# Splitting a 3136-point transform as 49 by 64 instead of 56 by 56 in a spectral layer with a gated feed-forward network

## The chip, the cores and the metric

The kernel runs on one core of a Trainium2 chip. The metric is the device time of one execution in microseconds (us), as the median over several runs. Engines: TensorE (PE; its weight loads are PEld), VectorE (DVE), ScalarE (ACT), GpSimd (POOL), and SyncE (SP), which issues the DMAs.

## The reference

The input x is 8 batches x 3136 positions x 256 channels, in float32. The output has the same shape.

```python
X = np.fft.rfft(x, axis=1)                  # along the 3136 positions
Yr = Xr @ w_r - Xi @ w_i + b_r              # complex 256 x 256 mix of the channels
Yi = Xr @ w_i + Xi @ w_r + b_i
Y = sign(Y) * max(abs(Y) - 0.01, 0)         # soft threshold, real and imaginary part apart
y = np.fft.irfft(Y, n=3136, axis=1)
h = max(y @ w_in, 0)                        # 256 -> 1024
c = depthwise 3-tap convolution of h along the positions (conv_w)
out = (h * sigmoid(c)) @ w_out              # 1024 -> 256
```

The feed-forward weights come as 64-bit floats. The kernel reads them as pairs of 32-bit words and makes two float32 parts of each.

## The kernel before

The transform over 3136 positions is done as two shorter ones, R = 56 rows by 56 columns. Row n, column j is position 56 n + j. *Stage 1* transforms over the rows, *stage 2* over the columns, *mix* multiplies the channels by the complex matrix, *shrink* is the soft threshold, *stage 3* goes back over the columns and *stage 4* over the rows. All of them are matmuls on TensorE except shrink.

**The two units of work.** A *piece* is the work of stage 1 (or of stage 4) on four columns of the first half with their four partners of the second half (`JC = 4`), so 56/8 = 7 pieces a batch and 56 in all. A *unit* is four of a batch's indices u (`UG = 4`); the real input leaves U = 28 indices, so 7 units a batch and 56 in all. Index 0 is special, since it is its own mirror image: in the kernel before it is packed with the other self-mirrored frequency as a unit member with 57 rows instead of 56.

**The way of the data.** A piece of x is loaded by two DMAs of 56 rows x 1024 floats (`load_x`, tile `xr`), goes through `quads` (four matmuls, each on one quadrant of the array: 64 rows by 64 columns), is copied to `a1` by ACT and DVE, and is stored to a scratch in DRAM, `sc1`. A unit is loaded from there (`load_a2`, tile `a2`, 112 rows), goes through `stage2` (8 matmuls), which writes a high part `fh` and a low part `fl`; `third` makes the third column of both (ACT and POOL). `mix` has 36 matmuls over three combinations. `shrink` takes two ACT instructions and one on POOL. `stage3_pe` has 8 matmuls on quadrants; `stage3_out` copies the result to `z1` (ACT) and stores it to a second scratch, `sc2`. Stage 4 loads from it a piece of 8 columns (`load_z2`), runs 8 matmuls and copies a high and a low part to `yh` and `yl`, which the feed-forward stage reads. The profile often shows two records for one such matmul (16 for the 8 of stage 2).

**The order.** Up to the feed-forward stage the order of every engine is that of the code: one loop, `for it in range(n_it + LAG)`, in which iteration `it` does stage 3 of unit it - 4, a piece of stage 1 of a later batch, stage 2 of unit `it`, shrink of unit it - 2, `third` of unit `it`, and mix of unit it - 1. Ahead of the loop stands the *head*, which does the pieces of batch 0. The last iterations, from `n_it` on, are the *drain*: no new units come. In five iterations near the end and in two of the drain a stage 4 of batch 0 is done (`Y0`, `Y1`), so that the feed-forward stage can start. All DMAs are issued by SP, in the order of the code; a DMA that has to wait holds up those behind it. The generator `later()` (`background`) loads and splits the weights of the feed-forward stage during the loop, a few instructions each iteration. It also loads the table of stage 4 (`i2`, from `in_inv`) and the three convolution taps (`cw`, by `load_bits`, L244 before). `load_inv1` loads the tables of stage 3, `load_t2` those of stage 2, `load_mix` the mixing weights `wm_raw`.

At a *batch boundary* the first unit of a batch needs the last piece of that batch: its store to `sc1`, then the load of `a2`.

The feed-forward stage goes over all positions in pieces of 448 columns: `up` (L542), relu (L544), taps (L547 to L551), sigmoid (L552), gate (L553 to L557), `down` (L570), and the store. The stage-4 pieces of batches 1 to 7 run between its matmuls. There a scheduler sets the order.

Of the kernel before, what the change touches and what calls it, by code (L numbers as in the profile page):

```python
# [18 lines left out]
R = 56  # L19
U = 28  # L20
SL = 57
SP = 64
H = 28
LAM = 0.01
UG = 4
NG = U // UG
JC = 4
P = 128
# [6 lines left out]
def _tables():  # L35
    n = np.arange(R)
    u = np.arange(U)

    f = np.zeros((R, 2, U))
    ang = 2 * np.pi * ((n[:, None] * u[None, :]) % R) / R  # L40
    f[:, 0, :] = np.cos(ang)
    f[:, 1, :] = -np.sin(ang)
    f[:, 1, 0] = np.where(n % 2 == 0, 1.0, -1.0)
    fwd1 = np.zeros((2, SP, SP))
    fwd1[:, :R, :R] = f.transpose(0, 2, 1).reshape(R, R)

    fwd2 = np.zeros((2, R, U, 2, SP))
    inv1 = np.zeros((U, 2, SP, SP))
    jj = np.arange(1, H)
    for uu in range(U):  # L50
        for s in range(SL):
            if uu == 0:
                c = 0 if s < 29 else 1
                k = R * s if s < 29 else 28 + R * (s - 29)
                th = 2 * np.pi * ((k * n) % S) / S
                sn, cs = np.sin(th), np.cos(th)
                edge = k in (0, S // 2)
                if edge:
                    sn = np.zeros(R)
                    cs = np.round(cs)  # L60
                w = 1.0 if edge else 2.0
                fwd2[c, :, 0, 0, s] = cs
                fwd2[c, :, 0, 1, s] = -sn
                inv1[0, 0, s, c:R:2] = w * cs[:H]
                inv1[0, 1, s, 2 + c:R:2] = w * sn[jj]
                if c == 0:
                    inv1[0, 0, s, R] = w * cs[H]
                else:
                    inv1[0, 1, s, 1] = w * sn[H]
            elif s < R:  # L70
                k = uu + R * s
                th = 2 * np.pi * ((k * n) % S) / S
                sn, cs = np.sin(th), np.cos(th)
                sg = 1.0 if k <= S // 2 else -1.0
                fwd2[0, :, uu, 0, s] = cs
                fwd2[1, :, uu, 0, s] = sn
                fwd2[0, :, uu, 1, s] = -sn * sg
                fwd2[1, :, uu, 1, s] = cs * sg
                for c, q in ((0, 1.0), (1, sg)):
                    inv1[uu, c, s, 0] = q  # L80
                    inv1[uu, c, s, 1] = q * (1.0 if s % 2 == 0 else -1.0)
                    inv1[uu, c, s, 2:R:2] = q * cs[jj]
                    inv1[uu, c, s, 3:R:2] = q * sn[jj]

    inv2 = np.zeros((2, 2, 2, U, 2, R))
    for h in range(2):
        for uu in range(U):
            for first in range(2):
                o = inv2[first, :, :, uu, h]
                m = n + (h if not first else 0)  # L90
                if uu == 0:
                    alt = np.where(m % 2 == 0, 1.0, -1.0)
                    if first:
                        o[0, h], o[1, h] = ((1.0, alt), (1.0, -alt))[h]
                        if h:
                            o[0, 0], o[1, 0] = 0.0, 0.0
                            o[0, 1], o[1, 1] = 1.0, -alt
                        else:
                            o[0, 0], o[1, 0] = 1.0, alt
                            o[0, 1], o[1, 1] = 0.0, 0.0  # L100
                    else:
                        sgn = (-1.0, 1.0)[h]
                        o[0, 0], o[1, 0] = 1.0, alt
                        o[0, 1], o[1, 1] = sgn, sgn * alt
                else:
                    th = 2 * np.pi * ((uu * m) % R) / R
                    if first:
                        th = th + h * 2 * np.pi * uu / (2 * R)
                        o[h, 0], o[h, 1] = 2 * np.cos(th), -2 * np.sin(th)
                    else:  # L110
                        sgn = (-1.0, 1.0)[h]
                        o[0, 0], o[1, 0] = 2 * np.cos(th), sgn * 2 * np.sin(th)
                        o[0, 1], o[1, 1] = -2 * np.sin(th), sgn * 2 * np.cos(th)
    order = [g * UG + 2 * k + kk for g in range(NG) for kk in range(2) for k in range(UG // 2)]
    inv2 = inv2[:, :, :, order] / S

    return {
        "fwd1": fwd1.reshape(2 * SP, SP).astype(np.float32),
        "fwd2": fwd2.reshape(2, 2, H, U * 2 * SP).transpose(0, 2, 1, 3).reshape(2 * R, U * 2 * SP).astype(np.float32),
        "inv1": inv1.reshape(U // 2, 2, 2, SP, SP).transpose(1, 3, 0, 2, 4).reshape(2 * SP, U * SP).astype(np.float32),  # L120
        "inv2": inv2.transpose(1, 2, 3, 0, 4, 5).reshape(2 * R, 2 * 2 * R).astype(np.float32),
    }
# [3 lines left out]
def spectral_ffn_kernel(ctx: ExitStack, tc: tile.TileContext, x, w_r, w_i, b_r, b_i,  # L126
                        w_in, conv_w, w_out, fwd1, fwd2, inv1, inv2, out):
    nc = tc.nc
    K1, K2 = 2 * R, 2 * SP

    dram = ctx.enter_context(tc.tile_pool(name="dram", bufs=1, space=DRAM))
    sc1 = [dram.tile([R, 2 * H, D], F32, name=f"sc1_{b}") for b in range(B)]
    sc2 = [dram.tile([H, 4, U, D], F32, name=f"sc2_{b}") for b in range(B)]
# [52 lines left out]
    with ExitStack() as ab:  # L186
# [13 lines left out]
        t2 = c1.tile([K1, U, K2], F32, name="t2")  # L200
# [4 lines left out]
        inv1v = inv1.rearrange("p (u c m) -> p u c m", u=U // 2, c=2)  # L205
        fwd2v = fwd2.rearrange("p (u m) -> p u m", u=U)
# [8 lines left out]
        def load_t2(g):  # L215
            nc.sync.dma_start(t2[:, g * UG:(g + 1) * UG, :], fwd2v[:, g * UG:(g + 1) * UG, :])
# [62 lines left out]
        def later():  # L279
# [12 lines left out]
            bits = [load_bits(conv_w[k].rearrange("(f p) w -> p f w", p=P), NF, "cw", bufs=1, tag=f"cw{k}") for k in range(3)]  # L292
            ask(0)
            yield None
            for n in range(len(pieces)):
                if n + 1 < len(pieces):
                    ask(n + 1)
                yield from split_weight(*asked.pop(0))
# [4 lines left out]
        def load_x(pool, b, jc, **kw):  # L303

            xr = pool.tile([P, JC, D], F32, name="xr", **kw)
            xv = x[b].rearrange("(n h j) d -> h n j d", h=2, j=H)
            for h in range(2):
                nc.sync.dma_start(xr[SP * h:SP * h + R], xv[h, :, jc * JC:(jc + 1) * JC, :])  # L308
# [9 lines left out]
        def store_a1(b, jc, a1):  # L318
            dst = sc1[b].rearrange("m (c r j) d -> r c m (j d)", r=2, j=4)
            for r in range(2):  # L320
                nc.sync.dma_start(dst[r, jc], a1[SP * r:SP * r + R].rearrange("p j h d -> p (j h d)"))
# [15 lines left out]
        def load_a2(b, g):  # L337
            a2 = a2p.tile([K1, UG, D], F32, name="a2")
            ld = nc.sync.dma_start(a2, sc1[b].rearrange("(u c) j d -> (c j) u d", c=2)[:, g * UG:(g + 1) * UG, :])
            return a2  # L340

        def stage2(g, a2):
# [3 lines left out]
            for t in range(NT):  # L346
                ps = psx.tile([P, UG, 2, SP], F32, name="ps_s2", tag="bank")
                for k in range(UG):
                    nc.tensor.matmul(ps[:, k], a2[:, k, t * P:(t + 1) * P], t2[:, g * UG + k, :],  # L349
# [34 lines left out]

        def shrink(v):
# [6 lines left out]
        def stage3_pe(g, r):  # L392
            ps = psa.tile([P, 2, UG // 2, D], F32, name="ps_s3")
            for k in range(UG // 2):
                for h in range(2):
                    for c in range(2):
                        rows = slice(SP * h, SP * (h + 1))
                        nc.tensor.matmul(ps[SP * c:SP * (c + 1), h, k, :], i1[rows, g * UG // 2 + k, c, :], r[rows, c, k, :],  # L398
                                         start=(k == 0), stop=(k == UG // 2 - 1), skip_group_check=True)
            return ps  # L400

        def stage3_out(b, g, ps):
            z1 = io.tile([P, 2, UG // 2, D], F32, name="z1", bufs=2)
            nc.scalar.copy(z1, ps)
            z1 = z1.rearrange("p h k e -> p (h k) e")
            dst = sc2[b].rearrange("j (a c) u e -> c (j a) u e", c=2)[:, :, g * UG:(g + 1) * UG, :]
            nc.sync.dma_start(dst[0], z1[0:R])
            if g == 0:
                nc.sync.dma_start(dst[1, 1:], z1[SP + 1:SP + R])
                nc.sync.dma_start(dst[1, 0:1, 1:], z1[SP:SP + 1, 1:])  # L410
                nc.sync.dma_start(dst[1, 0:1, 0:1], z1[R:R + 1, 0:1])
            else:
                nc.sync.dma_start(dst[1], z1[SP:SP + R])
# [5 lines left out]
        items = [(b, g) for b in range(B) for g in range(NG)]  # L419
        n_it = len(items)  # L420
        WP0, LAG, EXTRA = NG, 4, (3,)
        xs, vs, ss, xq = {}, {}, {}, []
        p1 = nx = NG
# [207 lines left out]
```

## Time and profile before

| | us |
|---|---|
| runs of the kernel before | 1701.3, 1705.64, 1705.16 (median 1705.16) |
| profiled execution, its own time | 1706.47 |
| its span in the profile | 1704.7 |
| PE busy in it | 1677.6 (98%) |
| DVE busy | 1400.5 (82%) |
| ACT busy | 1203.2 (71%) |
| mixing stage (stages 1 to 3 and mix), about | 0 to 507 |
| feed-forward stage, about | 507 to 1705 |

The profile's times are those of one execution. The page gives for each engine its busy time, share and number of instructions; the *chain* is the work that ended last, followed back from the last instruction through what released each step, so the shares on it say which engine sets the end. In a group's row the part after the bar is the busy time, the mean of one instruction in ns, and the idle time of the engine ahead of it with what ended it. DMA share is the mean busy share of the core's 16 DMA engines. PEclk is the granted TensorE clock as a part of full speed.

### The profile page before, as it was taken

How to read it: one execution, taken by the hardware profiler on the slowest of the kernel's cores; microseconds unless marked ns; L12 is line 12 of the kernel's file. 1: busy time of each engine (PE TensorE's matmuls, PEld its weight loads, DVE VectorE, ACT ScalarE, POOL GpSimd, SP SyncE). 2: the span in 40 equal slices, each digit the busy share in tenths (PEclk: the TensorE clock that was granted, in tenths of full speed). 3: DMA queues.
4: the chain of work that ended last, by engine and by line, in shares of the span. 5: the costliest groups of instructions: out<-in, count | busy, mean ns of one | idle time of the engine just before them, and what ended most of it. 6: DMA issues, size and time to landing. Idle time of an engine off the chain costs nothing.

```text
span 1704.7 us, 30596 instructions
## 1 busy us (share of the span) xinstructions
PE 1677.6 (98%) x12544; PEld 1554.2 (91%) x12544; DVE 1400.5 (82%) x1737; ACT 1203.2 (71%) x1604; POOL 209.9 (12%) x116
## 2 busy tenths in 40 slices
PE   6999999999999999999999999999999999999998
PEld 2878888888989999999999999999999999999998
DVE  2678989776649888888888888888888888888887
ACT  2667777777767777777776777677767777767676
POOL 0344454444430000000000000000000000000000
PEclk9999999999999999999999999999999999999999
DMA  9998888777731111110110011111101111000001
GB/s 249 259 272 250 248 234 253 230 229 200 193 96 36 44 44 33 44 55 33 55 55 33 24 54 55 33 55 55 33 23 55 55 34 55 33 23 22 22 22 44
DMA packets 109002, 163.77 MB, mean 96 GB/s; under 512 B 10680, under 2 KB 87728, under 8 KB 108864
## 3 DMA queue, kind: packets, MB, share of 16 engines
q1 hardware_dynamic: 108864, 161.83, 32.3%
q8 instruction: 99, 1.62, 0.4%
q14 instruction: 39, 0.32, 0.1%
HBM read 84.73 MB, written 77.07 MB: 95 GB/s over the span
## 4 chain that ended last, share of the span: by engine, by line
PE 96%; DMA 2%; ACT 1%; SPq 1%; issue 0%; DVE 0%; POOL 0%; ACTq 0%; DVEq 0%; POOLq 0%
PE ps_h L542 32%; PE acc L570 32%; PE ps_mx L377 13%; PE ps_s L349 7%; PE ps_s L171 6%; PE ps_s L398 3%; PE ps_s L316 3%; DMA a<-sc 1%; DMA xr<-in_x_dram 1%; DMA sc<-a 0%; DMA wm_raw<-in_w_i_dram 0%; SPq L244 0%; DMA sc<-ha 0%; ACT yh L180 0%; SPq L308 0%
## 5 line engine op out<-in xcount | busy, mean ns | idle before, releaser
L570 PE MATMUL acc<-wout,gh 128*128 128x256 f32 x3136 | 569.3, 281 | 0.5 <-ACT gh L556 0.5
L551 DVE SCALAR_TENSOR_TENSOR c<-h,cw,c 128x896 f32<-128x896 f32 x448 | 512.1, 1147 | 49.7 <-ACT c L549 47.6
L542 PE MATMUL ps_h<-yh,win 128*128 128x450 f32 x1792 | 548.9, 367 | 0.0
L570 PEld LDWEIGHTS acc<-wout,gh 128*128 128x128 f32 x3136 | 493.0, 188 | 6.9 <-ACT gh L556 0.7
L570 PE MATMUL acc<-wout,gl 128*128 128x256 f32 x1568 | 435.9, 280 | 0.0
L544 ACT ACTIVATE h<-ps_h 128x900 f32<-128x900 f32 x224 | 207.1, 924 | 243.5 <-PE ps_h L542 242.1
L542 PEld LDWEIGHTS ps_h<-yh,win 128*128 128x128 f32 x1792 | 338.2, 189 | 25.9 <-issue 0.4
L542 PE MATMUL ps_h<-yl,win 128*128 128x450 f32 x896 | 329.2, 367 | 0.0
L557 DVE TENSOR_TENSOR gl<-c,gh 128x896 fp32r<-128x896 f32 x224 | 242.7, 1088 | 67.9 <-ACT gh L556 65.2
L570 PEld LDWEIGHTS acc<-wout,gl 128*128 128x128 f32 x1568 | 293.3, 188 | 0.5
L553 DVE TENSOR_TENSOR c<-h,c 128x896 f32<-128x896 f32 x224 | 243.3, 1086 | 23.6 <-ACT c L552 23.2
L556 ACT CAST gh<-c 128x896 fp32r<-128x896 f32 x224 | 210.0, 941 | 42.1 <-DVE c L553 42.1
L552 ACT ACTIVATE c<-c 128x896 f32<-128x896 f32 x224 | 213.2, 952 | 27.1 <-DVE c L551 23.5
L377 PE MATMUL ps_mx<-wmix_hi,fh 128*128 128x256 f32 x672 | 193.6, 288 | 0.0
L377 PE MATMUL ps_mx<-wmix_hi,fl 128*128 128x256 f32 x672 | 188.7, 281 | 1.8 <-POOL fl L361 1.8
L377 PE MATMUL ps_mx<-wmix_lo,fh 128*128 128x256 f32 x672 | 188.8, 281 | 0.0
L542 PEld LDWEIGHTS ps_h<-yl,win 128*128 128x128 f32 x896 | 169.0, 189 | 10.9
L549 ACT ACTIVATE c<-h,cw 128x896 f32<-128x896 f32 x168 | 175.9, 1047 | 1.9
L389 POOL TENSOR_TENSOR r<-r,v 128x1024 f32<-128x1024 f32 x56 | 133.5, 2384 | 253.1 <-ACT v L388 245.3
L349 PEld LDWEIGHTS ps_s<-t,a 112*128 112x128 f32 x896 | 107.5, 196 | 57.4 <-issue 52.8
L349 PE MATMUL ps_s<-t,a 112*128 112x128 f32 x896 | 118.3, 287 | 14.3 <-DMA a<-sc 13.4
L377 PEld LDWEIGHTS ps_mx<-wmix_hi,fl 128*128 128x128 f32 x672 | 127.6, 190 | 2.0 <-POOL fl L361 2.0
(75 smaller groups left out, 1711.5 us busy)
## 6 DMA issues: line engine op xcount, KB each, us to landing
xr<-in_x_dram SPq DMA_DIRECT2D x112, 224.0 KB
a<-sc SPq DMA_DIRECT2D x56, 448.0 KB
z<-sc SPq DMA_DIRECT2D x56, 448.0 KB
out_dram<-o SPq DMA_DIRECT2D x27, 896.0 KB
sc<-z SPq DMA_DIRECT2D x104, 224.0 KB
sc<-a SPq DMA_DIRECT2D x98, 224.0 KB
sc<-ha SPq DMA_DIRECT2D x14, 224.0 KB
win_bits<-in_moe_w_in_dram SPq DMA_DIRECT2D x4, 512.0 KB
```

The lines of the kernel that those rows point to most:

```text
L349: nc.tensor.matmul(ps[:, k], a2[:, k, t * P:(t + 1) * P], t2[:, g * UG + k, :], start=(k == 0), stop=(k == UG - 1), skip_group_check=True)
L377: nc.tensor.matmul(ps[c][:, k, :], lt, rh, start=(n == 0), stop=(n == len(mm) - 1))
L389: nc.gpsimd.tensor_tensor(r, r, v, op=ALU.subtract)
L542: nc.tensor.matmul(ps[:, a, 0:CH + 2], lt, rh, start=(n == 0), stop=(n == len(mm) - 1))
L544: nc.scalar.activation(h, ps[:, :, 0:CH + 2], AF.Relu)
L549: nc.scalar.mul(c, h[:, :, 0:CH], cw[:, 0, f:f + 1])
L551: nc.vector.scalar_tensor_tensor(c, h[:, :, k:k + CH], cw[:, k, f:f + 1], c, op0=ALU.mult, op1=ALU.add)
L552: nc.scalar.activation(c, c, AF.Sigmoid)
L553: nc.vector.tensor_tensor(c, h[:, :, 1:CH + 1], c, op=ALU.mult)
L556: nc.scalar.copy(gh, c)
L557: nc.vector.tensor_tensor(gl, c, gh.bitcast(F32), op=ALU.subtract)
L570: nc.tensor.matmul(acc[m // 2][:, m % 2, :], lt[:, sl], rh[:, f, :], start=(f == 0 and n == 0 and m % 2 == 0), stop=(f == NF - 1 and n == ...
```

## The change

The transform is split as R = 49 rows by C = 64 columns. 49 is odd, so only index 0 is its own mirror image, and U = 24 full indices are left: 6 units a batch. Index 0 of four batches (`BH = 4`) forms one unit of its own (`g == NG`), with 64 rows in stage 2 and half of the array's columns in stage 3 (L406 after). So there are 50 units and 64 pieces (8 a batch); a piece of stage 4 has 98 rows and 98 columns instead of 112. Rows are moved as 48 and 1: two DMAs of 48 rows and one of two rows, for x and for `a1`; row 48 goes to a scratch of its own, `sc0`. `a2` has 128 rows, `z1` 64 in each half.

```diff
-R = 56
-U = 28
+R = 49
+C = 64
+U = (R - 1) // 2
+RU = 2 * U
+BH = 4
...
             for h in range(2):
-                nc.sync.dma_start(xr[SP * h:SP * h + R], xv[h, :, jc * JC:(jc + 1) * JC, :])
+                nc.sync.dma_start(xr[SP * h:SP * h + RU], xv[h, 0:RU])
+            nc.sync.dma_start(xr[RU:P:SP], xv[:, RU])
...
+        def store_a1(b, jc, a1, all_rows=True):
             for r in range(2):
-                nc.sync.dma_start(dst[r, jc], a1[SP * r:SP * r + R].rearrange("p j h d -> p (j h d)"))
+                nc.sync.dma_start(dst[r, jc], a1[SP * r:SP * r + RU].rearrange("p j h d -> p (j h d)"))
+            dst = sc0[b // BH][b % BH].rearrange("(c r j) d -> c r (j d)", r=2, j=4)
+            nc.sync.dma_start(dst[jc], a1[RU:P:SP].rearrange("p j h d -> p (j h d)"))
```

The pieces of stage 1 no longer come one an iteration. A table sets how many there are:

```diff
-        WP0, LAG, EXTRA = NG, 4, (3,)
+        LAG, WP0, LATE = 4, 8, 10
+        count = {1: 1, 2: 2, 3: 2, 4: 2, 5: 1, 6: 2, 7: 1, 8: 2, 9: 1, 10: 2}
-            n_s1 = min(1 + (it in EXTRA), n_it - p1)
+            n_s1 = min(count.get(it, (2, 1, 1, 2, 1, 1)[it % 6]) if it else 0, n_pc - p1)
```

One place of the steady loop, on PE (the same iteration's matmuls; `r`, `xr` and `a` are the inputs of stage 3, stage 1 and stage 2). Before:

```order
L398 MATMUL ps_s_2076<-r,i_273 64x256 x8
L316 MATMUL ps_s_2085<-xr,f_114 64x512 x2
L316 MATMUL ps_s_2086<-xr,f_114 64x512 x2
L349 MATMUL ps_s_2108<-t_115,a_1861 128x128 x4
L349 MATMUL ps_s_2117<-t_115,a_1861 128x128 x4
```

After:

```order
L403 MATMUL ps_s_2200<-r,i_275 64x256 x8
L306 MATMUL ps_s_2209<-xr,f_116 64x512 x2
L306 MATMUL ps_s_2210<-xr,f_116 64x512 x2
L306 MATMUL ps_s_2215<-xr,f_116 64x512 x2
L306 MATMUL ps_s_2216<-xr,f_116 64x512 x2
L347 MATMUL ps_s_2251<-t_117,a_2090 128x128 x4
L347 MATMUL ps_s_2260<-t_117,a_2090 128x128 x4
```

Two pieces of stage 1 stand between stage 3 and stage 2 in this iteration, where one stood.

The convolution taps are asked for later, at the third to fifth piece of weights, and the load of a batch's first `a2` follows right behind the store that it needs:

```diff
-            bits = [load_bits(conv_w[k]...) for k in range(3)]
+            bits = []
...
+                if 2 <= n < 5:
+                    bits.append(load_bits(conv_w[n - 2]..., tag=f"cw{n}"))
...
             for ps in ps1:
-                stage1_out(*items[p1], ps)
+                stage1_out(*divmod(p1, NX), ps)
                 p1 += 1
+            ask_a2(it + 1)
```

SP at the first batch boundary (`in_moe_conv_w` are the taps, `in_inv` 112x224 is the table of stage 4, `win_bits` the first weights of the feed-forward stage). Before:

```order
L407 DMA sc_0_65<-z_715 56x1024
L413 DMA sc_0_65<-z_715 56x1024
L291 DMA i_76<-in_inv_dram 112x224
L244 DMA cw_bits<-in_moe_conv_w_dram 128x8x2 x3
L244 DMA win_bits<-in_moe_w_in_dram 128x1024
L321 DMA sc_1_58<-a_728 56x1024 x2
L308 DMA xr<-in_x_dram 56x1024 x2
L239 DMA i_273<-in_inv_dram 128x256
L339 DMA a_808<-sc_1_58 112x4x256
L339 DMA a_810<-sc_1_58 112x4x256
```

After:

```order
L418 DMA sc_0_67<-z_745 64x1024 x2
L311 DMA sc_1_60<-a_749 48x1024 x2
L315 DMA sc_0_57<-a_749 2x1024
L334 DMA a_755<-sc_1_60 128x4x256
L297 DMA xr<-in_x_dram 48x1024 x2
L298 DMA xr<-in_x_dram 2x1024
L226 DMA i_275<-in_inv_dram 128x256
L334 DMA a_833<-sc_1_60 128x4x256
L334 DMA a_835<-sc_1_60 128x4x256
L418 DMA sc_0_67<-z_858 64x1024 x2
L278 DMA i_78<-in_inv_dram 98x196
L231 DMA win_bits<-in_moe_w_in_dram 128x1024
```

The store of `a` and the load of the next `a` moved ahead of the table, the weights and x; the taps moved out of this place.

In the head, x row 48 of all columns is loaded once and the mixing weights are asked for behind the last store instead of in the middle:

```diff
-                if jc == 3:
-                    raw = load_mix()
                 if jc == 5:
                     load_t2(0)
-            split_mix(raw)
+            raw = load_mix()
+            ask_a2(0, 1)
             load_t2(1)
             fetch(1)
+            split_mix(raw)
+            nc.sync.dma_start(hr, ah[RU:P:SP].rearrange("p c j h d -> p c (j h d)"))
```

Stage 3 runs over the column half `a` outside:

```diff
-            for k in range(UG // 2):
-                for h in range(2):
-                    for c in range(2):
+            for a in range(2):
+                for k in range(UG // 2):
+                    for h in range(2):
```

In the drain, the threshold is done on DVE (`clip`: v minus v clamped to ±λ, two instructions), `third` of the last unit stands ahead of it, and stage 4 is done in four drain iterations and four before:

```diff
-        Y0, Y1 = n_it - NPC - 2, n_it - 3
+        Y0, Y1 = n_it - 6, n_it - 1
+            if it == n_it - 1:
+                xs[it] = third(xs[it])
             if 0 <= it - 2 < n_it:
-                ss[it - 2] = shrink(vs.pop(it - 2))
+                ss[it - 2] = (clip if drain else shrink)(vs.pop(it - 2))
-            if it < n_it:
+            if it < n_it - 1:
                 xs[it] = third(xs[it])
-            if Y0 < it < Y1 or n_it < it <= n_it + 2:
+            if Y0 < it < Y1 or n_it <= it < n_it + LAG:
```

PE at the end of the drain, up to the first `up` matmul (`z` is the input of stage 4, `yh` that of `up`). Before:

```order
L171 MATMUL ps_s_6107<-i_76,z_5592 128x2x56 x3
L171 MATMUL ps_s_6107<-i_76,z_5592 128x112
L171 MATMUL ps_s_6116<-i_76,z_5592 128x2x56 x3
L171 MATMUL ps_s_6116<-i_76,z_5592 128x112
L398 MATMUL ps_s_6125<-r,i_273 64x256 x8
L542 MATMUL ps_h<-yh,win_78 128x450
```

After:

```order
L406 MATMUL ps_s_5809<-r,i_275 64x256 x8
L157 MATMUL ps_s_5824<-i_78,z_5698 128x2x49 x3
L157 MATMUL ps_s_5824<-i_78,z_5698 128x98
L157 MATMUL ps_s_5833<-i_78,z_5698 128x2x49 x3
L157 MATMUL ps_s_5833<-i_78,z_5698 128x98
L572 MATMUL ps_h<-yh,win_80 128x450
```

The last stage 3 stood directly ahead of the first `up`; now it is the index-0 unit's, and the last stage 4 stands between.

More of the change, by code (lines that the diff above doesn't have):

```diff
@@ L36, in _tables @@
     n = np.arange(R)
[L37 to L43, printed above, removed]
-    fwd1 = np.zeros((2, SP, SP))
[L45 to L67, printed above, removed]
-                else:
[L69 to L83, printed above, removed]
@@ L85, in _tables @@
-    inv2 = np.zeros((2, 2, 2, U, 2, R))
-    for h in range(2):
[L87 to L113, printed above, removed]
@@ L114, in _tables @@
-    order = [g * UG + 2 * k + kk for g in range(NG) for kk in range(2) for k in range(UG // 2)]
-    inv2 = inv2[:, :, :, order] / S
+    j = np.arange(C)
+    jj = np.arange(1, H)
+    s = np.arange(C)
+    f = np.zeros((R, R))
+    for u in range(1, U + 1):
+        ang = 2 * np.pi * ((n * u) % R) / R
+        f[:, 2 * u - 2], f[:, 2 * u - 1] = np.cos(ang), -np.sin(ang)
+    f[:, RU] = 1.0
+    fwd1 = np.zeros((2, SP, SP))
+    fwd1[:, :R, :R] = f
+    fwd2 = np.zeros((2, C, U + 1, 2, C))
+    inv1 = np.zeros((U // 2 + 1, 2, 2, C, C))
@@ new lines, in _tables @@
+    for u in range(1, U + 1):
+        k = u + R * s
+        th = 2 * np.pi * ((k[None, :] * j[:, None]) % S) / S
+        sn, cs = np.sin(th), np.cos(th)
+        sg = np.where(k <= S // 2, 1.0, -1.0)
+        i = u - 1
+        fwd2[0, :, i, 0], fwd2[1, :, i, 0] = cs, sn
+        fwd2[0, :, i, 1], fwd2[1, :, i, 1] = -sn * sg, cs * sg
+        for c, q in ((0, np.ones(C)), (1, sg)):
+            o = inv1[i // 2, c, i % 2]
+            o[:, 0] = q
+            o[:, 1] = q * np.where(s % 2 == 0, 1.0, -1.0)
+            o[:, 2::2] = q[:, None] * cs[jj].T
+            o[:, 3::2] = q[:, None] * sn[jj].T
@@ new lines, in _tables @@
+    for q in range(H + 1):
+        th = 2 * np.pi * ((R * q * j) % S) / S
+        edge = q in (0, H)
+        sn, cs = (np.zeros(C), np.round(np.cos(th))) if edge else (np.sin(th), np.cos(th))
+        w = 1.0 if edge else 2.0
+        fwd2[0, :, U, 0, q] = cs
+        fwd2[0, :, U, 1, q] = -sn
+        inv1[U // 2, 0, :, q, 0] = w
+        inv1[U // 2, 0, :, q, 1] = w * cs[H]
+        inv1[U // 2, 0, :, q, 2::2] = w * cs[jj]
+        inv1[U // 2, 1, :, q, 3::2] = w * sn[jj]
+    inv2 = np.zeros((2, 2, R, 2, R))
@@ new lines, in _tables @@
+    order = [g * UG + 2 * k + kk for g in range(NG) for kk in range(2) for k in range(UG // 2)]
+    for first in range(2):
+        for h in range(2):
+            sgn = (-1.0, 1.0)[h]
+            o = inv2[first, :, :, h]
+            m = n + (h if not first else 0)
+            for pos, i in enumerate(order):
+                u = i + 1
+                th = 2 * np.pi * ((u * m) % R) / R
+                if first:
+                    th = th + h * 2 * np.pi * u / (2 * R)
+                    o[h, pos], o[h, U + pos] = 2 * np.cos(th), -2 * np.sin(th)
+                else:
+                    o[0, pos], o[1, U + pos] = 2 * np.cos(th), sgn * 2 * np.cos(th)
+                    o[0, U + pos], o[1, pos] = -2 * np.sin(th), sgn * 2 * np.sin(th)
+            if first:
+                o[h, RU] = 1.0
+            else:
+                o[0, RU], o[1, RU] = 1.0, sgn
@@ L383, in mix, with clip @@
             return v
+        def clip(v):
+            r = wk.tile([K2, 2, UG // 2, D], F32, name="r", bufs=3)
+            nc.vector.tensor_scalar(r, v, LAM, -LAM, op0=ALU.min, op1=ALU.max)
+            nc.vector.tensor_tensor(r, v, r, op=ALU.subtract)
+            return r
         def shrink(v):
@@ L417, in spectral_ffn_kernel, with ask_a2 @@
         nc.scalar.activation(warm, warm, AF.Sigmoid)
[L419 to L423 removed]
+        items = [(b, g) for h in range(B // BH) for b, g in [(h * BH + b, g) for b in range(BH) for g in range(NG)] + [(h * BH, NG)]]
+        n_it, n_pc = len(items), B * NX
+        LAG, WP0, LATE = 4, 8, 10
+        count = {1: 1, 2: 2, 3: 2, 4: 2, 5: 1, 6: 2, 7: 1, 8: 2, 9: 1, 10: 2}
+        xs, vs, ss, a2s, xq = {}, {}, {}, {}, []
+        p1 = nx = NX
         def fetch(n):
             nonlocal nx
[L427 to L428 removed]
+            while len(xq) < n and nx < n_pc:
+                xq.append(load_x(s1p, *divmod(nx, NX), bufs=XRB))
                 nx += 1
+        def ask_a2(*its):
+            for i in its:
+                if i < n_it and i not in a2s:
+                    b, g = items[i]
+                    if p1 >= NX * (b + (1 if g < NG else BH)):
+                        a2s[i] = load_a2(b, g)
         ab.enter_context(tc.manual_schedule())
@@ L475, in spectral_ffn_kernel @@
         for it in range(n_it + LAG):
+            drain = it >= n_it
             fetch(XRB)
@@ L478, in spectral_ffn_kernel @@
                 load_t2(it + 1)
+            elif it == LATE:
+                load_t2(NG)
+                load_inv1(NG)
             if 0 <= it - 2 < NG:
                 load_inv1(it - 2)
-            for i in (it + 1, it + 2):
-                if i < n_it and i not in a2s and (i == it + 1 or i % NG):
-                    a2s[i] = load_a2(*items[i])
+            ask_a2(it + 1, it + 2)
             if it >= LAG:
@@ L522, in spectral_ffn_kernel @@
                 vs[it - 1] = mix(xs.pop(it - 1))
+        assert p1 == n_pc and not z2s and next(background, True)
     wk, hp, io, y_b = pool("cwk"), pool("chp", 3), pool("cio"), pool("y_b")
```

117 lines of the change are left out of this document (67 added, 50 removed).

## The prediction

> **What bounds the kernel now.** I read the page's busy table and its chain first: is one engine the bound from end to end?
>
> ```profile
> span 1704.7 us, 30596 instructions
> PE 1677.6 (98%) x12544; PEld 1554.2 (91%) x12544; DVE 1400.5 (82%) x1737; ACT 1203.2 (71%) x1604; POOL 209.9 (12%) x116
> PE 96%; DMA 2%; ACT 1%; SPq 1%; issue 0%; DVE 0%; POOL 0%; ACTq 0%; DVEq 0%; POOLq 0%
> ```
>
> TensorE is busy for 98% of the span and the chain of waits lies on it for 96%. So matmul time decides, and then the 27 us in which TensorE stands still. Next the windows, to see where it stands (columns: us, busy time of each engine, granted clock, DMA share, GB/s):
>
> ```profile
> 28.00:60.00 32.00, 25.14 (x188) 20.52 (x189) 15.65 (x28) 13.83 (x28) 6.18 (x4) 1.00 1.00 242
> 91.00:98.00 7.00, 5.91 (x28) 5.94 (x29) 2.04 (x4) 2.94 (x6) 0.00 (x0) 0.51 1.02 289
> 98.00:106.00 8.00, 8.00 (x77) 6.80 (x77) 6.73 (x11) 4.90 (x9) 3.64 (x2) 1.00 0.98 308
> 100.00:420.00 320.00, 320.00 (x3019) 272.36 (x3019) 264.29 (x460) 236.77 (x365) 150.46 (x80) 1.00 0.82 239
> 1000.00:1600.00 600.00, 600.00 (x4124) 577.94 (x4123) 521.82 (x545) 431.94 (x534) 0.00 (x0) 1.00 0.13 40
> ```
>
> In the long windows after 100 us TensorE is never idle, neither in the mixing stage nor in the feed-forward stage. The idle time lies ahead of 100 us, where the DMA share is 1.00, and at the change of stages (the drain, below). In the steady mixing stage the DMA share is 0.82, so there is some room, not much.
>
> **Price of a unit.** The chain in order of time (start, us, what), one unit with a piece of stage 1, and stage 4 of a later one:
>
> ```profile
> 101.03 1.02 PE ps_s L398 x16
> 102.06 0.86 PE ps_s L316 x8
> 102.92 1.98 PE ps_s L349 x16
> 104.90 4.20 PE ps_mx L377 x36
> ...
> 444.74 1.77 PE ps_s L171 x16
> ```
>
> A unit costs 1.02 (stage 3) + 1.98 (stage 2) + 4.20 (mix) = 7.20 us, a piece of stage 1 0.86, a piece of stage 4 1.77.
>
> **The change, part by part.**
>
> *Fewer units.* 8 batches x 7 = 56 become 8 x 6 + 2 = 50. Six fewer: 6 x 7.20 = -43.2. A unit still holds 512 columns of spectrum, so its mix and stage 2 keep their price.
>
> *More pieces of stage 1.* 64 instead of 56. The head takes 8 instead of 7 and waits for DMA there anyway; the loop takes 56 instead of 49: 7 x 0.86 = +6.0.
>
> *More pieces of stage 4.* 64 instead of 56, each with 98 moving columns instead of 112. Are they cheaper? The timeline of TensorE's weight loads:
>
> ```profile
> 442.68 1.86 PEld L349 LDWEIGHTS ps_s<-t,a 112*128 112x128 f32 x16 [0.39 <-issue]
> 444.46 1.87 PEld L171 LDWEIGHTS ps_s<-i,z 112*128 112x128 f32 x16
> ```
>
> Stage 2 moves 128 columns per matmul, stage 4 moves 112, yet sixteen weight loads take 1.86 and 1.87 us. The weight load sets the pace, not the columns, so I take 1.77 unchanged: 8 x 1.77 = +14.2. By columns it would be 1.55 a piece (rival 3). One of the eight falls in the mixing stage, seven in the feed-forward stage, where the window 1000 to 1600 shows no idle TensorE to hide them.
>
> *The two units of index 0.* They fill half of stage 3's four quadrants. Stage 3 alone, in short windows (us, PE busy, PEld busy, clock, DMA share, GB/s):
>
> ```profile
> 262.28:262.33 0.05, 0.04 (x4) 0.04 (x4) 1.00 1.65 615
> 262.33:262.55 0.22, 0.22 (x4) 0.17 (x8) 1.00 0.81 326
> 262.55:262.60 0.05, 0.05 (x8) 0.04 (x4) 1.00 0.81 328
> ```
>
> Four matmuls start within 0.05 us, the next four some 0.25 us later: four quadrants side by side, 16 in four rounds of 1.02/4 = 0.255. Index 0 has two quadrants, so eight rounds: +1.02 each, +2.0.
>
> *Sum of matmul work:* -43.2 + 6.0 + 14.2 + 2.0 = -21.0.
>
> *Stage 3's order.* It now issues one column half for all four matmuls, then the other. The trace shows four running side by side though the program lists eight matmuls and the profile records sixteen, so waiting ones do not hold up the other quadrants: 0. If they did (rival 2), 7 rounds instead of 4. The Trainium skill ("TensorE: Matmul & The Clock Gate", "Part 3: Packing small matmuls — row/col tiling") says that matmuls start and end strictly in program order. By that rule the new order would be rival 2, at 1719; the four that start together speak neither clearly for it nor against it.
>
> *First batch boundary and the taps.* The chain and the waits view (us in all, times, longest):
>
> ```profile
> 75.94 0.67 SPq L291
> 76.66 1.07 SPq L244
> ...
> 80.75 0.36 SPq L321
> 81.16 6.51 DMA sc<-a
> 87.75 4.21 DMA a<-sc
> 92.09 3.75 PE ps_s L349 x16
> 95.85 5.18 PE ps_mx L377 x36
> PE ps_s L349 <- DMA a<-sc: 13.4, 2, 10.5
> ```
>
> The inverse table (L291), three taps and the first weights (L244) were issued from 75.94 us, ahead of the last a1 store at 80.75. Then come the store, the load, and stage 2 and mix at half clock (0.51 in the window 91 to 98). 13.4 - 10.5 = 2.95 us of the wait are this boundary's, and the low clock costs (3.75 - 1.98) + (5.18 - 4.20) = 2.75: 5.7 us. The change takes those five loads out from in front of the store. But units 2 to 4 now carry two pieces each, with 0.40 MB in and 0.40 MB out per piece. A unit then moves 2.5 to 3.0 MB (a2 0.52, z none to 0.52, two pieces 1.60, tables 0.3) in 7.20 + 2 x 0.86 = 8.9 us: 283 to 342 GB/s, where the windows up to 106 us show 242 to 308. At 275 GB/s (their middle) 3.0 MB takes 10.9 us: 2 us late, for some four units: I take 8 us for this stretch. Lowest 3 (308 GB/s throughout: 0.8 us a unit), highest 14 (242: 3.5 us a unit). Against 5.7 before: +2.3 (-2.7 to +8.3).
>
> *Steady DMA.* Before, a unit moves 4 x 0.459 + 0.105 of weights = 1.94 MB in 8.06 us, 241 GB/s; the window says 239. After: a2 0.52 and z 0.52, 1.33 pieces x 0.80, weights 0.12: 2.24 MB in 7.20 + 1.33 x 0.86 = 8.35 us, 268 GB/s. Share 0.82 at 239 scales to 291 at 1.00, so I book 0; rival 1 is the other reading. What becomes late first is the a2 load behind a stage-2 matmul.
>
> *More DMA issues.* SP issues 13 instead of 9.4 transfers a unit: rows moved as 48 and 1, times 1.33 pieces. Its waits and one issue:
>
> ```profile
> 200.34 0.38 SPq L413 DMA_DIRECT2D sc<-z  x1
> SPq L407 <- ACT z L404: 179.8, 52, 8.3
> ```
>
> SP waits 179.8/52 = 3.5 us a unit for z; 3.6 more issues x 0.38 = 1.4 us fit into that: 0. Behind SP's wait stand the a1 stores and the next a2 load; once the room is gone they come late as in rival 1.
>
> *The head.* Chain before 34 us:
>
> ```profile
> 18.28 5.44 DMA wm_raw<-in_w_i_dram
> 24.65 3.37 DMA sc<-ha
> 28.10 5.79 DMA a<-sc
> ```
>
> The mixing weights stood in front of the last stores; now they come behind. One transfer of 5.44 us leaves the chain, but an eighth piece and the row-48 load are added, and all share one full set of queues. I take -1; bounds -4 (most of the 5.44) and +3 (the eighth piece, 0.8 MB at 242 GB/s).
>
> *The drain.* Chain and waits:
>
> ```profile
> 492.44 1.28 POOL fl L361
> 493.77 5.79 PE ps_mx L377 x34
> ...
> 505.75 0.69 ACT yh L180 x2
> PE ps_mx L377 <- POOL fl L361: 1.8, 1, 1.8
> PE ps_s L398 <- ACT yh L180: 0.9, 1, 0.9
> ```
>
> Last mix waits 1.8, runs 5.79 instead of 4.20 (1.6), and the last stage 3 waits 0.9: 4.3 us. The change puts `third` of the last unit ahead of a shrink, moves the shrink's work from POOL and ACT to DVE, and gives each of four drain steps a stage 4. All three gaps should close. New: the last stage 4 stands right ahead of the first `up` matmul, which then waits for its evacuation, two copies like the 0.69 above: 1.3. Net -3.0; bounds -4.3 and +1 (DVE, at 264/320 = 83%, late with the clip).
>
> *Together:* -21.0 + 2.3 + 0 + 0 - 1.0 - 3.0 = -22.7. The profiled execution took 1706.5 (span 1704.7 and 1.8 around it), 1.3 above the median of the runs, 1705.2. 1706.5 - 22.7 = 1683.8; against the median 1682.5.
>
> **The rivals.**
>
> 1. *Transfers bound the mixing stage.* For it: the window 28 to 60 shows a share of 1.00 at just 242 GB/s. Against it: 289 and 308 in the two windows after 91. At 250 GB/s a unit of 2.24 MB takes 8.96, 0.61 more than its matmuls; over the 38 units that carry all traffic +23, so 1705.7. At 242 it is 0.91 x 38 = +34, so 1717. It decides below 268 GB/s.
>
> 2. *The other side: stage 3 goes serial.* If a waiting matmul holds up the ones behind it, the second column half starts only in the first half's last round: 7 rounds for 4, 3 x 0.255 = 0.77 a unit, x 48 = +36.7, so 1719. The gain is gone from 0.47 us a unit. Against it stand the four that start together.
>
> 3. *Cheaper pieces.* Stage 4 by columns: 64 x 1.77 x 98/112 instead of 64 x 1.77 is -14, so 1668. Against it are the two equal weight-load rows. Or transfers of 48 and 64 rows run at a higher rate than those of 56: a seventh more rate on rows of x, a1 and z, some two thirds of the bytes, is a tenth over all: 275 becomes 302 GB/s, 3.0 MB take 9.9 us, 1 us late instead of 2, so 4 us instead of 8 at the boundary, and the head's 30 us of transfers lose 3: 1675.5. No row tells rates by row count apart. The Trainium skill ("DMA: Bandwidth & Descriptors", "Why a DMA increments its semaphore by 16 and not by 1") says that a transfer is spread over the largest number of engines, up to 16, that divides its slowest dimension: 14 for 56 rows, 16 for 48 and 64. That would make this rival, an estimate from the page, which no run here shows.
>
> **How the numbers follow.** The sum stands: 0.60 (the bounds of boundary, head and drain add up to -9 and +14; two thirds of that, since they hardly all fall one way, is 1676 to 1692). A transfer bound in part only, 1692 to 1700: 0.08. Rival 1 in full: 0.14, of it 0.10 near 250 GB/s and within 0.3%, 0.04 nearer 242 and past 1710. Rival 2: 0.06, all slower. Rival 3: 0.12, half on each of its two forms. A third of a per cent is about what this measurement tells from no change: 1700.0 and 1710.3. Faster: 0.60 + 0.08 + 0.12 = 0.80. Within: the 0.10 of rival 1. Slower: its 0.04 and 0.06 of rival 2. Range 1668 to 1700: it ends above at the partial transfer bound and leaves out 0.20.
>
> **What would show each step.** Right: 50 groups of 36 mix matmuls at 4.20; units 7.20 us apart without a piece and 8.06 with one; stage 4 still 1.77 per 16; stage 3 still 1.02 and about 2.04 for index 0; in the steady windows some 265 GB/s and TensorE without idle time; the drain's three waits gone and one of about 1.3 ahead of the first `up`. Wrong: stage 2 waits for a2 unit after unit with the clock falling to 0.5 (rival 1); stage 3 near 1.8 (rival 2); stage 4 near 1.55 (rival 3); waits of more than 14 us in the first 110 us. Most open is the stretch from 60 to 110 us, which I sized with a mean rate.

## The result, and the profile after

The changed kernel took 1690.9 us in the median of its first four runs (1687.7 to 1693.0) and 1689.2 in four later ones; the kernel before took 1705.0 beside the first four and 1704.1 beside the later ones. The ratio is 0.992 (95% interval 0.990 to 0.994): faster, by 14 to 15 us where I had forecast 22.7. The page's first lines of the changed kernel's profile:

```profile
span 1685.9 us, 30291 instructions
PE 1656.4 (98%) x12328; PEld 1534.7 (91%) x12328; DVE 1391.8 (83%) x1719; ACT 1173.4 (70%) x1578; POOL 183.6 (11%) x102
PE 95%; DMA 2%; ACT 1%; DVE 1%; SPq 1%; issue 1%; POOL 0%; ACTq 0%; DVEq 0%; POOLq 0%
```

TensorE lost 21.2 us of busy time (1677.6 to 1656.4), as the sum of matmul work said (-21.0). It stands still for 29.5 us instead of 27.1. The windows show where (columns as in the prediction):

```profile
0.00:28.00 28.00, 16.36 (x64) 4.38 (x64) 5.62 (x10) 6.17 (x10) 0.20 (x4) 0.80 0.78 225
28.00:60.00 32.00, 23.06 (x160) 18.81 (x160) 17.15 (x29) 13.19 (x24) 6.16 (x4) 0.75 0.90 264
110.00:140.00 30.00, 27.34 (x239) 22.98 (x239) 25.34 (x42) 20.80 (x32) 12.37 (x7) 0.94 0.90 272
140.00:200.00 60.00, 60.00 (x565) 50.41 (x565) 52.15 (x88) 43.94 (x68) 26.68 (x15) 1.00 0.94 281
200.00:300.00 100.00, 100.00 (x933) 83.71 (x932) 87.61 (x147) 73.49 (x116) 46.36 (x24) 1.00 0.92 268
1000.00:1600.00 600.00, 600.00 (x4129) 577.89 (x4129) 517.67 (x547) 425.91 (x532) 0.00 (x0) 1.00 0.12 39
```

In the steady stage the transfers run at 268 to 281 GB/s (forecast 268) with a share of 0.92 to 0.94, and TensorE has no idle time. The loss lies in the start-up, which now reaches to 140 us: TensorE is idle for 20.6 of the first 60 us (16.6 before), and again from 110 to 140, where it never was before. The clock of 0.75 to 0.80 in the first two rows can't be held against the kernel before: the 1.00 of its window 28 to 60 rests on clock records that start only at 39.85 us, and its first stage 2, at 33.98 us, took 3.75 us for 16 records as the changed kernel's first did. The chain in order of time gives the prices (start, us, what), here a steady unit, the pair of pieces in one unit, and a unit with stage 4:

```profile
70.03 1.98 PE ps_s L347 x16
72.01 4.20 PE ps_mx L375 x36
76.21 1.04 PE ps_s L403 x16
77.25 0.86 PE ps_s L306 x8
...
121.44 1.72 PE ps_s L306 x16
...
445.45 1.76 PE ps_s L157 x16
```

All are as forecast but stage 3, which takes 1.04 instead of 1.02. Ninety-eight moving columns cost 1.76 us a piece where 112 cost 1.77, and the sixteen weight loads of a piece take 1.87 us as before: the columns do not set the price, which fits the weight load's pace.

The table sets the profiled executions of this study side by side (from TensorE's timeline; idle time counts gaps of over 0.1 us between the first mix and the first `up`).

| kernel | first matmul | first mix | first `up` | idle between |
|---|---|---|---|---|
| before | 4.5 | 42.4 | 507.5 | 6.6 |
| before, second profile | 4.5 | 42.6 | 503.0 | 4.6 |
| changed | 7.9 | 44.8 | 475.7 | 4.7 |
| changed, second profile | 7.8 | 42.1 | 475.5 | 7.3 |
| weights in the middle (e2) | 7.3 | 43.0 | 482.3 | 9.9 |
| row 48 split (e3) | 5.5 | 41.5 | 474.9 | 6.8 |
| both head edits (e4) | 5.7 | 40.3 | 476.8 | 9.4 |
| three a1 buffers (e5) | 7.6 | 42.5 | 475.7 | 5.2 |
| x as 49 rows (e6) | 7.5 | 42.5 | 492.9 | 13.7 |
| stage 3 in the old order (e7) | 7.6 | 42.6 | 479.7 | 9.5 |
| old drain (e8) | 7.5 | 43.1 | 479.4 | 8.1 |
| taps early (e10) | 7.4 | 43.6 | 482.6 | 10.5 |
| deeper buffers (e11) | 5.6 | 38.3 | 473.6 | 9.6 |
| before, two drain parts (e12) | 4.5 | 40.1 | 502.2 | 5.2 |

From the first `up` to the last matmul both profiles of before take 1192.9, both of the changed kernel 1205.8. In these two pairs all that differs between executions of one kernel lies ahead of the first `up`.

### The profile page after: what moved, and what is told of

Same layout as the page of the kernel before. It is cut to its first block, busy times and chain, and to the rows that moved or that the text cites. A ratio compares the mean times of both kernels' runs of the same rounds, so it can differ in the third digit from the quotient of the medians.

```text
span 1685.9 us, 30291 instructions
## 1 busy us (share of the span) xinstructions
PE 1656.4 (98%) x12328; PEld 1534.7 (91%) x12328; DVE 1391.8 (83%) x1719; ACT 1173.4 (70%) x1578; POOL 183.6 (11%) x102
## 4 chain that ended last, share of the span: by engine, by line
PE 95%; DMA 2%; ACT 1%; DVE 1%; SPq 1%; issue 1%; POOL 0%; ACTq 0%; DVEq 0%; POOLq 0%
PE ps_h L572 33%; PE acc L600 33%; PE ps_mx L375 12%; PE ps_s L157 7%; PE ps_s L347 5%; PE ps_s L306 3%; PE ps_s L403 3%; DMA sc<-a 1%; DMA hx<-in_x_dram 1%; DMA t<-in_fwd_dram 0%; DMA xr<-in_x_dram 0%; SPq L461 0%; SPq L311 0%; POOL fl L359 0%; DMA sc<-ha 0%
## 5 line engine op out<-in xcount | busy, mean ns | idle before, releaser
L375 PE MATMUL ps_mx<-wmix_hi,fh 128*128 128x256 f32 x600 | 172.9, 288 | 0.0
L375 PE MATMUL ps_mx<-wmix_hi,fl 128*128 128x256 f32 x600 | 168.3, 281 | 2.7 <-POOL fl L359 2.7
L375 PE MATMUL ps_mx<-wmix_lo,fh 128*128 128x256 f32 x600 | 168.3, 280 | 0.0
L347 PEld LDWEIGHTS ps_s<-t,a 128*128 128x128 f32 (+1 forms) x800 | 96.3, 197 | 48.0 <-issue 24.6
L393 POOL TENSOR_TENSOR r<-r,v 128x1024 f32<-128x1024 f32 x48 | 114.4, 2384 | 229.0 <-ACT v L392 219.7
L157 PEld LDWEIGHTS ps_s<-i,z 98*128 98x128 f32 x1024 | 122.4, 192 | 2.8 <-DVE v L380 0.8
L157 PE MATMUL ps_s<-i,z 98*128 98x98 f32 x1024 | 123.5, 274 | 0.0
```

The lines of the kernel that those rows point to most:

```text
L157: nc.tensor.matmul(to, z2[:, j, t * P:(t + 1) * P], i2[:, 0 if jg or j else 1, :], start=(j == 0), stop=(j == JG - 1), skip_group_check=True)
L347: nc.tensor.matmul(ps[:, k], a2[0:kk, k, t * P:(t + 1) * P], t2[0:kk, q, :], start=(k == 0), stop=(k == UG - 1), skip_group_check=True)
L375: nc.tensor.matmul(ps[c][:, k, :], lt, rh, start=(n == 0), stop=(n == len(mm) - 1))
```

## The experiments

**The two kernels again.**

> The changed kernel again, unaltered, for its spread and a second profile. The four times on record go from 1687.7 to 1693.0, and the profiled one is the lowest of them. Theory A (the head is what I mis-sized: +3 instead of -1, the rest of the sum holds): the first mix again starts near 44.8 us, the drain ends near 476 to 480, the feed-forward stage takes 1209.6; time 1690 +- 2. Theory B (transfers in the loop bound it in part, differently from run to run): TensorE's waits between 60 and 200 us differ from the first profile's 4.7 us by 2 us or more, and the time follows them.

> The kernel before, unaltered, for a second profile: its profiled execution took 1706.5, 2.6 above the median of its 17 runs, the changed kernel's 1687.7 is below its own. Theory: what differs between executions of one kernel lies ahead of 160 us, where transfers are late by chance. Then the feed-forward stage takes 1197.1 again, the drain's three waits are 4 us again, and TensorE's idle time and low clock before 110 us differ by some 2 us. Rival: the spread lies everywhere (a slower feed-forward stage by 1 us or more).

The changed kernel took 1689.2 (ratio to before 0.9915, 0.9901 to 0.9929). Its first mix came at 42.1, not near 44.8, and the waits of the loop were 7.3, not 4.7, so neither theory had it whole: in these two profiles head and loop trade with each other, and the end of the stage is the same to 0.2 us. Both profiled executions were the fastest of their four, 3.2 and 1.8 us under the median, so the median execution loses some 2 to 3 us more than the profiles show; no profile shows where. The kernel before took 1702.7 (ratio 1.0002). Its second profile is what I lacked when I forecast. The chain at its first batch boundary:

```profile
79.67 0.35 SPq L321
...
80.07 4.34 DMA sc<-a
...
84.49 5.65 DMA a<-sc
...
90.27 2.02 PE ps_s L349 x16
92.30 4.20 PE ps_mx L377 x36
```

The reader should hold this against the same chain in the prediction. Here the store takes 4.34 instead of 6.51 (the load behind it 5.65 instead of 4.21), stage 2 waits 1.08 instead of 2.95, and it starts at full clock: 2.02 and 4.20 where it was 3.75 and 5.18. The two spans differ by 4.5 us (1704.7 and 1700.2), and this place accounts for (2.95 - 1.08) + 1.73 + 0.98 = 4.6 of it. The expectation of some 2 us was low; that the spread lies ahead of 110 us holds. The three taps stood in front of the store in both and held SP for 3.36 and 3.46 us, so they are not what differs. Nor is the long stall an exception: in e12, below, whose start-up code is that of the kernel before, stage 2 waited 3.63 us at this place and ran at half clock again.

**The head.**

```diff
 # e2: mixing weights in the middle, second table ahead of a2
+                if jc == 3:
+                    raw = load_mix()
...
-            raw = load_mix()
-            ask_a2(0, 1)
+            split_mix(raw)
             load_t2(1)
             fetch(1)
-            split_mix(raw)
+            ask_a2(0, 1)
 # e3: row 48 in two parts, six pieces ahead
             ask_x()
-            nc.sync.dma_start(xh[RU:P:SP], xv[:, RU])
-            for _ in range(3):
+            nc.sync.dma_start(xh[RU:P:SP, 0:2 * JC], xv[:, RU, 0:2 * JC])
+            for _ in range(2):
+                ask_x()
+            nc.sync.dma_start(xh[RU:P:SP, 2 * JC:], xv[:, RU, 2 * JC:])
+            for _ in range(3):
                 ask_x()
```

> The head's order of before for the mixing weights (asked in the middle, t2 of unit 1 ahead of a2), all else as changed. Theory A: the DMA queues had room in the head (share 0.10 and 0.39 in two slices before 30 us), so the weights cost nothing in the middle and the second unit's table no longer lands last (39.7 us): first mix 2 to 3 us earlier, time 1688 (-2 to -3 to the changed kernel). Theory B, or that what the head gains the first boundary takes back: within 1 us of the changed kernel.

> In the head, row 48 is loaded for the first two pieces alone and for the other six later, and six pieces are asked for ahead of the first store instead of four. Theory A: the first matmul waits for the two-row transfer (it landed at 7.76, the first piece at 4.98) and the queues then run dry to 10.7; first matmul at 5 to 6 us, no empty slice near 10 us, the last store of the head 2 to 3 us earlier, time 1688. Theory B: earlier head, but within 1 us of the changed kernel at the end.

> Both edits of the head together. Theory A: they act on different stretches and add: first mix at 40 to 41 us instead of 44.8, time 1686 (-4 to -5). Theory B: the loop's transfers are no earlier, the gain goes into waits between 60 and 140 us: within 1.5 us of the changed kernel.

e2 took 1694.1 (0.9936, 0.9923 to 0.9949), 3 to 5 us above the changed kernel's medians, where a gain or no change was expected; the intervals just overlap, so that it is slower is likely, not proved. e3 took 1686.9 (0.9901, 0.9886 to 0.9916), e4 1688.4 (0.9909, 0.9895 to 0.9922); against 0.9915 the intervals overlap, so a gain of 1 to 2 us is not proved. What row 48 did is seen in the chain of the changed kernel and in TensorE's first rows, of the changed kernel and of e3:

```profile
2.12 5.64 DMA hx<-in_x_dram
```

```profile
7.90 2.84 PE L306 MATMUL ps_s<-hx,f 49*64 49x512 f32 x12 [7.90 <-DMA hx<-in_x_dram]
```

```profile
5.48 3.00 PE L306 MATMUL ps_s<-hx,f 49*64 49x512 f32 x12 [5.48 <-DMA hx<-in_x_dram]
```

The first matmul waits for the two-row transfer of all columns, 3.4 us longer than before; with only the first two pieces' columns in front it waits to 5.48. But against e1 the first mix moves by 0.6 us and the first `up` by as much: the gain of 2.3 is spent on the way. e4 brings the first mix forward by 1.8 us against e1 and pays 2.1 more in waits. That fits theory B: the start-up is a stretch in which transfers set the pace, and an earlier head only waits later. It is not proved by one profile each, since one and the same head reaches its first mix at times that differ as much (44.8 and 42.1 in the changed kernel; 42.4, 42.6 and, in e12, 40.1 with the head of before). Why e2 alone is slower, if it is, I can't say; its waits lie at 56 and 90 us (3.2 and 3.6) and four smaller ones between 139 and 313.

**Buffers.** With two pieces in a unit, the chain of the changed kernel runs through a1:

```profile
103.11 4.34 DMA sc<-a
...
107.64 0.69 DVE a L319
...
109.39 0.68 DVE fl L353
...
114.35 1.73 POOL fl L359
116.12 4.28 PE ps_mx L375 x34
```

The copy into a1 waits for the store out of it; behind it on DVE stand the parts of stage 2, then POOL, then the mix. In e1, from 40 to 170 us (us in all, times, longest):

```profile
ACT a L318 <- DMA sc<-a: 13.0, 7, 3.3
```

```diff
 # e5                                        # e11: e3's head, e5, and
-name="a1", bufs=2)                          -DB, XRB, SL_ENG = 1, 3,
+name="a1", bufs=3)                          +DB, XRB, SL_ENG = 1, 4,
```

> A third buffer for a1, nothing else. Theory C (formed from e1 to e4): with two pieces a unit the copy of a piece into a1 waits for the store of the piece two before it to land; ACT and DVE stand in line (13.0 and 9.2 us from 40 to 170 us in e1), so stage 2's parts and with them the mix come late. With three buffers these waits fall below 3 us, TensorE's idle time between first mix and first up falls from 7.3 (e1) to 3 to 4, time -3 to -4 to the changed kernel, about 1686.5. Theory B (bandwidth): the transfers are late anyway, the waits move from a1 to a2 and x, time within 1 us.

> For a better version: the head of e3 (row 48 in two parts, six pieces ahead), three buffers for a1 and four for x. Theory B (after e5: one more buffer only moves the wait to x and a2): as e3, 1686 to 1688. Theory D (x was the next to wait in e5, 2.4 us, for lack of a buffer): the x wait near 56 us goes and nothing takes its place, 1683 to 1685.

In e5 the wait of a1 for its store is gone and no mix waits any more, but 1688.7 (0.9915, 0.9901 to 0.9928) is no gain. TensorE's waits of e5 in the same stretch, then those of e11:

```profile
PE ps_s L347 <- DMA a<-sc: 2.9, 1, 2.9
PE ps_s L306 <- DMA xr<-in_x_dram: 2.4, 1, 2.4
```

```profile
PE ps_s L347 <- DMA a<-sc: 8.6, 1, 8.6
PE ps_s L347 <- DMA t<-in_fwd_dram: 0.8, 1, 0.8
```

The waits moved to a2 and x, as theory B had it; the gain of 3 to 4 us that C forecast did not come: C falls. In e11 the x wait is gone too, the first mix starts at 38.3 instead of 42.1, and nearly all that was gained stands as one wait of 8.6 us for the a2 of batch 1, at 80 us. Theory D was right on the x wait and wrong that nothing takes its place; its first `up` still comes 1.9 us before e1's. e11 took 1685.1 (0.9898, 0.9882 to 0.9913), the lowest median here: clearly below the kernel before, while its interval still touches the changed kernel's.

**How a transfer is spread over engines.**

```diff
             for h in range(2):
-                nc.sync.dma_start(xr[SP * h:SP * h + RU], xv[h, 0:RU])
-            nc.sync.dma_start(xr[RU:P:SP], xv[:, RU])
+                nc.sync.dma_start(xr[SP * h:SP * h + R], xv[h, 0:R])
```

> In the loop, x is loaded as 49 rows by one transfer per half instead of 48 and a transfer of the two last rows. If a transfer is spread over the largest number of engines up to 16 that divides its rows (the trace counts 16, 15 and 3 semaphore steps for transfers of 48, 56 and 2 rows, one more than the engines where these are fewer than 16), 49 rows use 7 engines: those carry 1.70/16 + 0.535/7 = 0.183 MB a unit instead of 0.140, at 291/16 = 18.2 GB/s that is 10.0 us a unit instead of 8.35, over 38 units +60: 1730 to 1755. If the rows don't matter, two fewer issues a piece and the same bytes: 1687 to 1691.

1707.7 (1.0023, 1.0012 to 1.0034): this one edit takes back the whole gain of the change and more, 18 us. The semaphore steps of an x transfer in the trace are 8 for 49 rows, 16 for 48, 15 for 56, 3 for 2; by the rule in the expectation seven engines carry 49 rows. The trace does not name the engines of a transfer, so this stays an inference from the steps. From issue to landing the transfers of 48 rows take 4.23 us on average between 60 and 200 us in the changed kernel (44 of them), those of 49 rows 5.73 (42), those of 56 rows in the kernel before 5.94 (36). This time does not tell the engines apart either: 56 rows at fifteen steps took no less than 49 rows at eight. The size was a third of what I expected, since I took 291 GB/s for the limit of sixteen engines. The steady window of e6:

```profile
200.00:300.00 100.00, 97.66 (x884) 80.67 (x883) 84.64 (x141) 69.28 (x109) 42.54 (x22) 1.00 0.83 259
```

TensorE is idle for 2.3% of it. A unit so took some 8.55 us, in which seven engines, if it is seven, moved 0.183 MB each: an estimate of at least 21 GB/s an engine, not 18.2.

**Stage 3's order.**

```diff
-            for a in range(2):
-                for k in range(UG // 2):
-                    for h in range(2):
+            for k in range(UG // 2):
+                for h in range(2):
+                    for a in range(2):
```

> Stage 3 in the order of before (index, row half, column half) in the changed kernel. By my sum the order is worth 0: within 1 us, 1.02 to 1.04 for 16 records as before, 1.0 more for an index-0 unit. If matmuls of one quadrant hold up the others (rival 2), the old order is faster by up to 0.7 a unit; the changed kernel's profile shows 1.04 for 16, so I expect none of that.

1689.0 (0.9913, 0.9897 to 0.9929). The chain rows, of e7 and of the changed kernel:

```profile
209.46 1.02 PE ps_s L403 x16
```

```profile
208.70 1.04 PE ps_s L403 x16
```

Rival 2 falls: the order costs at most 0.02 us a unit, 1 us in 48; from one mix to the next, units with one piece are 8.08 us apart in the changed kernel and 8.07 in e7, which makes some 0.5. The rest of e7's profile holds a caution: one mix waited 1.8 us at 307 us, so not every stall lies in the start-up.

**The drain.**

```diff
 # e8, on the changed kernel
-                ss[it - 2] = (clip if drain else shrink)(vs.pop(it - 2))
+                ss[it - 2] = shrink(vs.pop(it - 2))
 # and third behind it for all units
 # e12, on the kernel before: clip (v minus v clamped, on DVE) for shrink where it >= n_it,
 # and third of the last unit ahead of it
```

> The drain's threshold back on ACT and POOL, and third of the last unit behind it; stage 4's new places stay. My sum gave the drain 3.0 us in all, of it 3.4 to third and the clock that falls while mix waits for it (1.8 + 1.6): mix waits 1.5 to 2 us for fl again, runs at half clock in part, time +2 to +3.5. Rival: the four drain steps with a stage 4 cover the shrink anyway, and third alone is what counts or neither: within 1 us.

> The kernel before with two parts of the change alone: third of the last unit ahead of the shrink, and the threshold on DVE in the drain; stage 4 stays at its old places. In e8 third behind the shrink cost nothing, since a stage 4 now stands in front of the last mix. Theory: without that stage 4 it does cost, so here the wait of 1.8 for fl and the mix at 5.79 for 4.20 go, -2 to -3.5, about 1701. Rival: clip only makes DVE late, and the gain is under 1.

e8 took 1690.5 (0.9918, 0.9906 to 0.9931), e12 1699.3 (0.998, 0.9969 to 0.999): -3.8 us against the kernel before, by the interval -1.7 to -5.3. The last two mixes in e12's chain, then the last mix in e8's and the one wait of its drain:

```profile
485.55 4.25 PE ps_mx L377 x36
...
490.82 4.41 PE ps_mx L377 x36
```

```profile
457.22 4.39 PE ps_mx L375 x36
```

```profile
PE ps_s L406 <- POOL r L393: 0.9, 1, 0.9
```

In e12 the wait of 1.8, the mix of 5.79 and the wait of 0.9 ahead of the last stage 3 are gone: from the start of the last-but-one mix to the first `up` it takes 16.9 us, where both profiles of before take 21.5. So the 4.3 that I gave the three gaps is about right, and it needs no new split; e12 does not tell the two edits apart. Against e12 the changed kernel is some 8 to 11 us faster by the medians and the ratios: that much is left to the split, the new order of transfers and the rest. In e8 the same edit undone leaves the mix at 4.39: a stage 4 in front of it covers `third`. What remains there is the wait of stage 3 for the threshold on POOL, 0.9, and +1.3 us in the median, inside the intervals.

**The taps.**

```diff
-            bits = []
+            bits = [load_bits(conv_w[k]...) for k in range(3)]
...
-                if 2 <= n < 5:
-                    bits.append(load_bits(conv_w[n - 2]...))
```

> The changed kernel with the three taps asked for at once again, ahead of the first weights. They now stand behind the batch's store and a2 load, so by my sum they cost at most their three issues on SP (3 x 0.4 to 1.4 us) in a stretch whose SP waits: 0 to +1. If tap loads in front are what cost the boundary (5.7 us before), +2 or more.

1693.2 (0.9944, 0.993 to 0.9958), some 4 us above the changed kernel by the ratios (0.992 and 0.9915); the interval just misses that of e1 and overlaps the wider one of the first four runs. SP's timeline in e10, and TensorE's waits there over the whole span:

```profile
93.33 5.92 SPq L231 DMA_DIRECT2D cw_bits<-in_moe_conv_w_dram  x3
```

```profile
PE ps_mx L373 <- POOL fl L357: 4.5, 3, 1.8
```

Three transfers of 8 KB hold SP for 5.92 us, not for the 1.2 to 4.2 that I allowed, and the a1 stores and x loads behind them come late; the mixes at 122, 141 and 160 us wait for their last part. "0 to +1" was too low.

## Why the prediction was right or wrong

- **Units, pieces, stage 4, stage 3's order, the steady transfers:** right, each within 0.1 us of its price. Rivals 1, 2 and the first half of 3 are excluded by the rows above. An index-0 stage 3 measured 1.95 in e8's chain (forecast 2.04). The feed-forward stage grew by 12.9 us, forecast 7 x 1.77 = 12.4.
- **The drain, -3.0:** the three gaps closed, as forecast, but the new wait of 1.3 ahead of the first `up` did not come: the waits view of the changed kernel has only 0.2 there, for the second copy. So the drain gave more than forecast; e12, without the new places of stage 4, shows -3.8 in the median and 4.7 in the profiles.
- **The step that failed: "First batch boundary", +2.3.** Its second half was near in size: the changed kernel's start-up in the loop loses 4.7 to 7.3 us of idle time and some 3 us by units above their usual price, 8 to 10 in two executions that were both faster than the median; I took 8. That is partly luck, since I had spread it as a late unit four times over: the losses are a wait of stage 1 near 59 us (0.85 and 3.8), one of 1.2 to 1.3 for a2 at the boundary, and mixes waiting for POOL from 116 us on. (The 283 to 342 GB/s of that working should read 281 to 337 for 2.5 to 3.0 MB in 8.9 us; nothing hangs on it.) The first half was wrong: "5.7 before" came from one execution, and in another the same place cost 1.1; in e12 it was as large again, and that execution too lay above its median, by 1.9. With 1.9 in place of 6.6 (this boundary and the 0.8 to 0.9 ahead of the second stage 2, which I had left out) the term is +6 to +8. The profiled execution that I started from, 1706.5, was 2.4 to 3.4 us above the later medians of its kernel (1704.1, 1703.9, 1703.0), and its excess over the second profile lay in the very place that the change was to mend: I booked it as gain.
- **The head, -1.0:** the sign did not hold. The first mix came 2.4 us later in one profile and 0.5 earlier in the other, with one piece of the loop's stage 1 (0.86) fewer ahead of it, so the term is +3.3 and +0.4; over all profiles here with either head it is about +1. The two-row transfer, which I named and did not price, delayed the first matmul by 3.4.
- **DMA issues at 0:** right for the steady stage. The engines' rule, which I put at a small chance as part of rival 3, fits what the Trainium skill says ("DMA: Bandwidth & Descriptors", "Why a DMA increments its semaphore by 16 and not by 1"): the steps agree for every row count here. e6 shows that without rows in 48 and 1 the gain of the change is gone. The faster transfers did not make the start-up shorter than forecast.

Taken together, -21.0, +0.5 for the feed-forward stage, up to +1 for stage 3, +7 for the start-up, -3.8 for the drain and up to +1 for the head is about -15 to -17; measured are -14 to -15 in the medians and -14.5 between the second profiles. Part of the rest can be found: with every unit at its usual length, the changed kernel's second profile still runs over by some 2 us after 165 us, in places of a few tenths each (the mixes at 403 and 410 us took 4.7 instead of 4.4), too short for the column of idle time. What remains stays open, as does e2.

## What to carry to other kernels

A stall in a start-up where transfers set the pace differs from one execution to the next: take its size from more than one profile before booking its removal. There, an earlier load or another buffer moved most of the wait to the next tile (e4, e5, e11), while the row count of a transfer was worth 18 us (e6); fewer bytes were not tried. Work that replaces idle time at a change of stages is worth trying alone: one reordering and a threshold on DVE gave 3.8 us without the new split.

## What the runs showed of the hardware that I had not expected

- The semaphore steps of a transfer follow its number of rows: 16 for 48, 64 and 128 rows, 15 for 56, 8 for 49, 12 for 55, 3 for 2. Loading 49 rows at once instead of 48 and 1 cost 18 us.
- A DMA share near 1 does not tell the bytes moved: windows with a share of 0.90 to 1.02 moved 242 to 308 GB/s.
- Three loads of 8 KB each in pieces of 8 bytes held SP for 5.92 us in e10, and for 3.36 and 3.46 in the two profiles of the kernel before.
